# Squared-relu attention before two feed-forward blocks: key blocks in pairs, chunk sums copied out apart

## The chip, the cores and the metric

The kernel runs on one core of a Trainium2 chip. The metric is the device time of one execution in microseconds (us); a difference of under 0.2% between two kernels is about what these measurements cannot tell from none.

## The reference

```python
scores = (1.0 / S) * np.matmul(z, z.transpose(0, 2, 1))   # z: 2 x 3008 x 64
attn = np.maximum(scores, 0.0) ** 2
x = u * np.matmul(attn, v)                                # u, v: 2 x 3008 x 256, fp32
x = x.reshape(6016, 256)
h = np.maximum(x @ w_in, 0.0);  x = h * h @ w_out         # 256 -> 2048 -> 256
h = x @ w2_in;  g = h - np.tanh(h);  y = g @ w2_out       # 256 -> 2048 -> 256
```

The weights of the two feed-forward blocks are float64, the rest is float32.

## The kernel before, in words

Every operand of a matmul is split into a rounded part (hi) and a remainder (lo), both in the type fp32r, and a product is three matmuls: hi by hi, lo by hi, hi by lo. The split of an activation is two passes: a cast or copy that writes hi, and a subtraction that writes lo.

Queries are cut into 12 chunks: per batch five of 512 and one of 448. The work is a list `steps`, and a step of attention is one chunk with one block of 128 keys (24 blocks a chunk, 288 steps; the last block has 64 keys, which lie twice, in the upper and in the lower 64 rows). Then come 192 steps "m1" and 192 steps "m2", for the first and the second feed-forward block (a chunk with 128 of the 2048 hidden columns): 21 of m1, then m2 and m1 in turn, at the end m2 alone. TensorE's array is split in attention into two halves of 64 rows that work side by side, on two blocks in the scores and on the two halves of a block's keys in the values. I call two such matmuls side by side a slot. A pair of blocks has 3 slots of scores and 12 of values.

`front(i)` does the first half of step i. For attention it computes the scores of two blocks at each even step (`two_scores`, L309), takes relu (L371) and square (L372) on ScalarE, makes hi by a cast on VectorE (L385) or, for every third block, on ScalarE (L381), and lo by a subtraction on VectorE (L386, L382). `back(n)` does the second half: for attention it adds the block's values to four sums, `o`, one PSUM bank each (L462): two halves of the rows by two halves of the 256 columns. After a chunk's last block it joins the sums. For each half d of the columns ScalarE copies one bank (L484), VectorE adds the other (L485) and multiplies by u (L486), and a DMA stores the result. The pool `po` has just these four banks, so that the next chunk's first matmuls wait until a bank has been read.

The order on every engine is written out by hand, in one loop: `front(n + LOOK)`, then `back(n)`, with LOOK = 3. Each engine works its queue off in this order.

Operands that have to be loaded and split (v, z, the weights, the stored x) are units in three `Lane`s. A unit has the step at which it is needed and one from which it may be loaded. `due(n)` forces what step n needs, `fill(n, k)` puts up to k passes between the passes of a step, and `pace(n)` works out k from what is left and when it is needed (at most 2 per block in attention, 4 in m1). A weight unit takes nine passes, six of them on VectorE (L181 to L194), a v unit two, a z unit four. All split v and weights live in the pool `wp` (32 buffers of 4 KB per partition, 24 of them first for v). PSUM has eight banks: four for `o`, four single ones for scores and hidden columns (`ps`).

Of the kernel before, what the change touches and what calls it, by code (L numbers as in the profile page):

```python
# [9 lines left out]
F32 = mybir.dt.float32  # L10
F32R = mybir.dt.float32r
# [22 lines left out]
def kernel(  # L34
# [8 lines left out]
    w2_out: bass.AP,  # L43
    yT: bass.AP,
):

# [35 lines left out]
    halves = (slice(0, DQK), slice(DQK, P))  # L82
# [14 lines left out]
    at = {s: i for i, s in enumerate(steps)}  # L97

    wt = {}
    zt = {}  # L100
# [160 lines left out]
    for b in range(B):  # L261
        base, end = at["att", b * NC, 0], at["att", (b + 1) * NC - 1, 0]
        for j in range(NV):
            w_units.append((base + 2 * j, load_v, split_v, (b, j), 2))
            free_w.append(end + 2 * j + 2)
        for t in range(NC):
            z_units.append((base + 4 * t, load_z, split_z, (b, t), 4))
            free_z.append(end + min(4 * t + 4, KB))
    for m in range(2):
        for f in range(NF):  # L270
            w_units.append((at[("m1", "m2")[m], 0, f], load_w, split_w, (m, f), 9))

    for units, free, slots, first in ((w_units, free_w, NW, 1), (z_units, free_z, NZ, 0)):
        for i, u in enumerate(units):
            start = free[i - slots] + LOOK if i >= slots else 1 if i == first + 1 else 0
            units[i] = (u[0], start, *u[1:])
    for c in range(NCH):
        need = at["m1", c, 0]
# [15 lines left out]


    pair = {}
    acc = {}
    score = {}

    def two_scores(i):  # L300

        for j in (i, i + 1):
            score[j] = ps.tile([P, NMAX], F32, tag="s", name="s")
        for t, (hk, hq) in enumerate(((0, 0), (1, 0), (0, 1))):
            for g, rows in enumerate(halves):
                _, c, k = steps[i + g]
                b, q, n = chunks[c]

                T.matmul(  # L309
                    score[i + g][:, :n],  # L310
                    lhsT=zt[b, k // 4][rows, hk ^ g, (k % 4) * P : (k % 4 + 1) * P],
                    rhs=zt[b, q // NMAX][rows, hq ^ g, :n],
                    start=t == 0,
                    stop=t == 2,
                )
    late = deque()
    calm = [0]
    for kind, _, _ in steps:
# [14 lines left out]
    def interleave(n, main, k):  # L333
# [10 lines left out]
            late.popleft()()  # L344
        fill(n, k)

    def front(i):
        kind, c, k = steps[i]
        b, q, n = chunks[c]
        if kind == "att":  # L350
            if i % 2 == 0:
                two_scores(i)
            s = score.pop(i)
        else:
            s = ps.tile([P, NMAX], F32, tag="s", name="s")
        a = ap_.tile([P, NMAX], F32, tag="a", name="a")
        s_, a_ = s[:, :n], a[:, :n]
        h = hp.tile([P, NMAX], F32R, tag="hi", name="hi")
        pair[i] = (h,)
        if kind != "att" or k < KB - 1:  # L360
            l = hp.tile([P, NMAX], F32R, tag="lo", name="lo")
            pair[i] = (h, l)
        if kind == "att":
            if k == 8:
                xt[c] = xp.tile([P, KD, NMAX], F32, tag="x", name="x")
                t0 = b * S + q
                SP.dma_start(
                    out=xt[c][:, :, :n],
                    in_=uT[:, t0 : t0 + n].rearrange("(k p) t -> p k t", p=P),
                )  # L370
            A.activation(a_, s_, AF.Relu, scale=scale)  # L371
            A.activation(a_, a_, AF.Square)  # L372
            if k == KB - 1:

                up = slice(TAIL, P)
                main = [
                    lambda: V.tensor_copy(h[:, :n], a_),
                    lambda: V.tensor_sub(h[up, :n], a[up, :n], h[up, :n]),
                ]
            elif k % 3 == 1 and c > 0:  # L380
                A.activation(h[:, :n], a_, AF.Copy)  # L381
                main = [lambda: V.tensor_sub(l[:, :n], a_, h[:, :n])]  # L382
            else:
                main = [
                    lambda: V.tensor_copy(h[:, :n], a_),  # L385
                    lambda: V.tensor_sub(l[:, :n], a_, h[:, :n]),  # L386
                ]
            interleave(i, main, 2 if c == 0 else min(1 + (k + 1) % 2, pace(i)))
            return
        m = 0 if kind == "m1" else 1  # L390
        w = wt["w", m, k]
        xh, xl = xs[m, c]
# [44 lines left out]
    def back(i):  # L437
        kind, c, k = steps[i]
        b, q, n = chunks[c]
        nk = KB if kind == "att" else NF  # L440
        if k == 0:
            acc[kind] = [
                po.tile([P, NMAX], F32, tag="o", name="o")
                for _ in range(KD * (2 if kind == "att" else 1))
            ]
        o = acc[kind]
        if kind == "att":
            w, c0 = wt["v", b, k // 2], (k % 2) * D
        else:
            w, c0 = wt["w", 0 if kind == "m1" else 1, k], KD * P  # L450
        got = pair.pop(i)
        terms = [(0, got[0]), (1, got[0])]
        if len(got) == 2:
            terms.append((0, got[1]))
        seq = [(j, d) for j in range(len(terms)) for d in range(KD)]
        if k in (0, nk - 1):
            seq.sort(key=lambda x: x[1])
        for j, d in seq:
            hl, mv = terms[j]
            if kind == "att":  # L460
                for g, rows in enumerate(halves):
                    T.matmul(  # L462
                        o[g * KD + d][:, :n],
                        lhsT=w[rows, hl, c0 + d * P : c0 + (d + 1) * P],
                        rhs=mv[rows, :n],
                        start=k == 0 and j == 0,
                        stop=k == nk - 1 and j == len(terms) - 1,
                    )
                continue
            T.matmul(  # L470
                o[d][:, :n],
                lhsT=w[:, hl, c0 + d * P : c0 + (d + 1) * P],
                rhs=mv[:, :n],
                start=k == 0 and j == 0,
                stop=k == nk - 1 and j == len(terms) - 1,
            )
        if k < nk - 1:
            return
        t0 = b * S + q
        if kind == "att":  # L480
            x = xt.pop(c)
            for d in range(KD):
                t = tp.tile([P, NMAX], F32, tag="t", name="half")
                A.activation(t[:, :n], o[d][:, :n], AF.Copy)  # L484
                V.tensor_add(t[:, :n], o[KD + d][:, :n], t[:, :n])  # L485
                V.tensor_mul(x[:, d, :n], t[:, :n], x[:, d, :n])  # L486
            SP.dma_start(out=xd[c, :, :, :n], in_=x[:, :, :n])
        elif kind == "m1":
            xh, xl = new_xs(1, c)
            for d in range(KD):  # L490
                A.activation(xh[:, d, :n], o[d][:, :n], AF.Copy)
                V.tensor_sub(xl[:, d, :n], o[d][:, :n], xh[:, d, :n])
        else:
            y = xp.tile([P, KD, NMAX], F32, tag="x", name="y")
            for d in range(KD):
                if d == 0 or c < NCH - 1:
                    A.activation(y[:, d, :n], o[d][:, :n], AF.Copy)
                else:
                    V.tensor_copy(y[:, d, :n], o[d][:, :n])
                if c == NCH - 1:  # L500
                    SP.dma_start(out=yT[d * P : (d + 1) * P, t0 : t0 + n], in_=y[:, d, :n])
            if c < NCH - 1:
                SP.dma_start(
                    out=yT[:, t0 : t0 + n].rearrange("(k p) t -> p k t", p=P), in_=y[:, :, :n]
                )


    with tc.manual_schedule():
        for n in range(-LOOK, len(steps)):
            i = n + LOOK  # L510
            if i < len(steps):
                due(i)
                front(i)
            while i >= len(steps) and late:
                late.popleft()()
            if n >= 0:
                back(n)


# [34 lines left out]
```

## Time and profile before

| | |
|---|---|
| time, 3 runs | 1584.35, 1586.05, 1586.63 us, median 1586.05 |
| profiled execution | 1589.54 us, its span 1587.5 us |
| TensorE (PE) busy | 1550.9 us, 98% |
| VectorE (DVE) busy | 1235.3 us, 78% |
| ScalarE (ACT) busy | 1150.8 us, 72% |
| mean granted TensorE clock | 0.983 |

The time of an execution is its span and some 2 us around it. PE is busy while any matmul is in flight, also at a lower clock. Of the engines' names, PEld is TensorE's loading of weights, SP the queue that issues most DMAs. "[1.67 <-ACT half L484]" behind an instruction is the idle time of its engine just before it and what ended it.

### The profile page before, as it was taken

How to read it: one execution, taken by the hardware profiler on the slowest of the kernel's cores; microseconds unless marked ns; L12 is line 12 of the kernel's file. 1: busy time of each engine (PE TensorE's matmuls, PEld its weight loads, DVE VectorE, ACT ScalarE, POOL GpSimd, SP SyncE). 2: the span in 40 equal slices, each digit the busy share in tenths (PEclk: the TensorE clock that was granted, in tenths of full speed). 3: DMA queues.
4: the chain of work that ended last, by engine and by line, in shares of the span. 5: the costliest groups of instructions: out<-in, count | busy, mean ns of one | idle time of the engine just before them, and what ended most of it. 6: DMA issues, size and time to landing. Idle time of an engine off the chain costs nothing.

```text
span 1587.5 us, 23868 instructions
## 1 busy us (share of the span) xinstructions
PE 1550.9 (98%) x8880; PEld 1295.7 (82%) x8880; DVE 1235.3 (78%) x2161; ACT 1150.8 (72%) x2032; POOL 24.2 (2%) x25
## 2 busy tenths in 40 slices
PE   8999999999999999999999999999999999999998
PEld 6777878777777978888888888888888888888887
DVE  7777767787756778987778788877778787778788
ACT  7788978888877867776766666666666676666676
POOL 0000000000000000000000000000000000000014
PEclk9999999999999999999999999999999999999999
DMA  4331003222000321000000000000000000000000
GB/s 127 113 101 54 15 28 95 69 67 67 28 27 2 105 92 54 1 27 1 16 10 1 27 1 27 1 27 1 25 1 27 1 26 1 1 14 1 14 1 25
DMA packets 32772, 52.38 MB, mean 33 GB/s; under 512 B 2960, under 2 KB 19600, under 8 KB 32656
## 3 DMA queue, kind: packets, MB, share of 16 engines
q1 hardware_dynamic: 32496, 50.60, 9.8%
q8 instruction: 69, 1.13, 0.3%
q14 instruction: 47, 0.39, 0.1%
q10 hardware_dynamic: 160, 0.26, 0.1%
HBM read 38.54 MB, written 12.32 MB: 32 GB/s over the span
## 4 chain that ended last, share of the span: by engine, by line
PE 89%; DVE 6%; ACT 4%; issue 1%; DMA 0%; SPq 0%; DVEq 0%; ACTq 0%
PE s L395 31%; PE o L470 31%; PE o L462 21%; PE s L309 6%; ACT a L371 1%; ACT a L372 1%; DVE half L485 1%; DVE a L427 1%; DVE lo L386 1%; DVE f L424 1%; DVE hi L385 0%; DVE x L486 0%; DVE a L420 0%; ACT hi L381 0%; DVE vw L127 0%
## 5 line engine op out<-in xcount | busy, mean ns | idle before, releaser
L462 PE MATMUL o<-hi,vw 64*128 64x512 f32 (+1 forms) x2304 | 399.0, 400 | 23.1 <-ACT half L484 13.8
L470 PE MATMUL o<-hi,ww 128*128 128x512 f32 (+1 forms) x1536 | 413.3, 386 | 2.6 <-ACT half L484 1.6
L395 PE MATMUL s<-xh,ww 128*128 128x512 f32 (+1 forms) x1536 | 405.1, 386 | 0.0
L462 PEld LDWEIGHTS o<-hi,vw 64*128 64x128 f32 x2304 | 286.8, 193 | 77.5 <-ACT half L484 21.8
L470 PEld LDWEIGHTS o<-hi,ww 128*128 128x128 f32 x1536 | 288.2, 188 | 57.6 <-ACT half L484 2.1
L395 PEld LDWEIGHTS s<-xh,ww 128*128 128x128 f32 x1536 | 288.1, 188 | 54.8 <-issue 0.6
L403 ACT ACTIVATE a<-s 128x512 f32<-128x512 f32 (+1 forms) x192 | 113.2, 589 | 189.2 <-PE s L395 187.8
L462 PE MATMUL o<-lo,vw 64*128 64x512 f32 (+1 forms) x1104 | 247.6, 393 | 0.1
L470 PE MATMUL o<-lo,ww 128*128 128x512 f32 (+1 forms) x768 | 241.3, 385 | 0.2 <-POOL lo L435 0.2
L410 DVE TENSOR_TENSOR lo<-a,hi 128x512 fp32r<-128x512 f32 (+1 forms) x192 | 130.6, 680 | 137.2 <-ACT hi L408 136.5
L395 PE MATMUL s<-xl,ww 128*128 128x512 f32 (+1 forms) x768 | 233.4, 385 | 0.0
L371 ACT ACTIVATE a<-s 128x512 f32<-128x512 f32 (+1 forms) x288 | 166.5, 578 | 70.0 <-PE s L309 59.3
L416 ACT ACTIVATE f<-s 128x512 f32<-128x512 f32 (+1 forms) x192 | 112.9, 588 | 120.7 <-PE s L395 120.7
L372 ACT ACTIVATE a<-a 128x512 f32<-128x512 f32 (+1 forms) x288 | 179.6, 624 | 9.4
L462 PEld LDWEIGHTS o<-lo,vw 64*128 64x128 f32 x1104 | 163.6, 190 | 19.5 <-DVE lo L386 1.2
L309 PE MATMUL s<-z 64*128 64x512 f32 (+1 forms) x864 | 165.8, 406 | 7.1 <-ACT z L145 4.6
L470 PEld LDWEIGHTS o<-lo,ww 128*128 128x128 f32 x768 | 144.0, 188 | 28.2 <-POOL lo L435 0.8
L395 PEld LDWEIGHTS s<-xl,ww 128*128 128x128 f32 x768 | 144.2, 188 | 26.9
L427 DVE COPY_PREDICATED a<-small,f 128x512 f32<-128x512 uint8 (+1 forms) x192 | 147.1, 766 | 6.2
L420 DVE TENSOR_TENSOR a<-s,a 128x512 f32<-128x512 f32 (+1 forms) x192 | 130.1, 677 | 15.3 <-ACT a L417 9.7
L309 PEld LDWEIGHTS s<-z 64*128 64x128 f32 x864 | 117.7, 198 | 23.3 <-ACT z L145 4.6
L424 DVE TENSOR_TENSOR f<-s,f 128x512 f32<-128x512 f32 (+1 forms) x192 | 130.7, 681 | 6.6
(47 smaller groups left out, 1458.8 us busy)
## 6 DMA issues: line engine op xcount, KB each, us to landing
wraw<-in_moe_w_in_dram SPq DMA_DIRECT2D x32, 256.0 KB, 2.9
wraw<-in_moe_w_out_dram SPq DMA_DIRECT2D x32, 256.0 KB, 3.2
vraw<-in_v_dram SPq DMA_DIRECT2D x22, 256.0 KB, 2.8
x<-in_u_dram SPq DMA_DIRECT2D x10, 512.0 KB, 4.8
xd<-x SPq DMA_DIRECT2D x10, 512.0 KB, 3.0
xr<-xd SPq DMA_DIRECT2D x10, 512.0 KB, 3.3
out_dram<-y SPq DMA_DIRECT2D x10, 512.0 KB, 2.8
zraw<-in_z_dram SPq DMA_DIRECT2D x18, 128.0 KB, 3.9
```

The lines of the kernel that those rows point to most:

```text
L309: T.matmul(score[i + g][:, :n], lhsT=zt[b, k // 4][rows, hk ^ g, (k % 4) * P : (k % 4 + 1) * P], rhs=zt[b, q // NMAX][rows, hq ^ g, :n], s ...
L371: A.activation(a_, s_, AF.Relu, scale=scale)
L372: A.activation(a_, a_, AF.Square)
L395: T.matmul(s_, lhsT=w[:, hl, kd * P : (kd + 1) * P], rhs=mv[:, kd, :n], start=j == 0, stop=j == len(seq) - 1,)
L403: A.activation(a_, s_, AF.Relu)
L410: main.append(lambda: V.tensor_sub(l[:, :n], a_, h[:, :n]))
L416: A.activation(f_, s_, AF.Tanh, scale=TB)
L420: lambda: V.tensor_sub(a_, s_, a_),
L424: lambda: V.tensor_mul(f_, s_, f_),
L427: late.append(lambda: V.copy_predicated(a_, small_, f_))
L462: T.matmul(o[g * KD + d][:, :n], lhsT=w[rows, hl, c0 + d * P : c0 + (d + 1) * P], rhs=mv[rows, :n], start=k == 0 and j == 0, stop=k == nk ...
L470: T.matmul(o[d][:, :n], lhsT=w[:, hl, c0 + d * P : c0 + (d + 1) * P], rhs=mv[:, :n], start=k == 0 and j == 0, stop=k == nk - 1 and j == le ...
```

## The change

A step of attention is now a pair of blocks (12 a chunk, 144 in all). The scores of a pair go to one tile of two PSUM banks, and one relu, one square, one cast (always on VectorE) and one subtraction work on both blocks (1024 elements per partition). The loop first emits the scores and relu of step n+2, then the values of step n, then square, cast and subtraction of step n+2. The last block's values take 3 slots in place of 4: one half of the array does one half of the columns.

After a chunk's last pair, ScalarE copies two banks into one tile and VectorE the other two into a second, at once; the addition of the two tiles and the multiplication by u go into the list `late`, whose entries are put ahead of the passes of the next pair's split (`interleave`, unchanged). The four tiles of this kind come from `wp`, of which 7 buffers are kept for them and for the pairs' tiles; therefore 12 weight units are now loaded ahead of the second batch's v, and of the other 20 one may be loaded when the first batch's v is freed, and 19 only from the last chunk of attention on. In m1 and m2, scores' banks and hi and lo are pair tiles of the same total size.

```diff
 LOOK = 3
+APART = 2
-READY = 3
+READY = 2
+NTEMP = 7
-    ps = ctx.enter_context(tc.tile_pool(name="ps", bufs=4, space=bass.MemoryType.PSUM))
+    ps = ctx.enter_context(tc.tile_pool(name="ps", bufs=2, space=bass.MemoryType.PSUM))
-    steps = [("att", c, k) for c in range(NCH) for k in range(KB)]
+    steps = [("att", c, p) for c in range(NCH) for p in range(NV)]
...
+    early = NW - NTEMP - NV - 1
+    w_units[NV:NV] = weights[:early]
+    w_units += weights[early:]
+    free_w += [at["m1", 0, 0]] * NTEMP
+    for units, free, slots, first in ((w_units, free_w, NW - NTEMP, 1), (z_units, free_z, NZ, 0)):
         for i, u in enumerate(units):
+            start = free[i - slots] + APART + 1 if i >= slots else 1 if i == first + 1 else 0
...
+    def scores(i):
...
+        s = ps.tile([P, 2, NMAX], F32, tag="s", name="s")
...  (six matmuls, as in two_scores)
+        a = wp.tile([P, 2, NMAX], F32, tag="w", name="a2")
+        A.activation(a[:, :, :n], s[:, :, :n], AF.Relu, scale=scale)
+        return a
+
+    def squares(i, a):
...
+        h = hp.tile([P, 2, NMAX], F32R, tag="h", name="h2")
+        l = wp.tile([P, 2, NMAX], F32R, tag="w", name="l2")
+        A.activation(a, a, AF.Square)
+        main = [
+            lambda: V.tensor_copy(h[:, :, :n], a),
+            lambda: V.tensor_sub(l[:, :, :n], a, h[:, :, :n]),
+        ]
+        interleave(i, main, min(5, pace(i)) if c else 4)
+
+    def values(i):
...
+        terms = ((0, h), (1, h), (0, l))
+        order = [(g, d, d) for g in range(2) for d in range(KD)]
+        if last:
+            order = [(1, 0, 1), (0, 0, 0), (0, 1, 1)]
...  (for each entry of order, for each term: one matmul per half of the rows)
+        e = [wp.tile([P, KD, NMAX], F32, tag="w", name="e") for _ in range(2)]
+        for d in range(KD):
+            A.activation(e[0][:, d, :n], o[d][:, :n], AF.Copy)
+            V.tensor_copy(e[1][:, d, :n], o[KD + d][:, :n])
+        def join():
+            V.tensor_add(e[0][:, :, :n], e[0][:, :, :n], e[1][:, :, :n])
+        def gate():
+            V.tensor_mul(x[:, :, :n], e[0][:, :, :n], x[:, :, :n])
+            SP.dma_start(out=xd[c, :, :, :n], in_=x[:, :, :n])
+        late.append(join)
+        late.append(gate)
...
-        for n in range(-LOOK, len(steps)):
-            i = n + LOOK
-            if i < len(steps):
+        for n in range(-1, len(steps)):
+            until = n + (APART if n + APART < at["m1", 0, 0] else LOOK)
+            todo = []
+            while ahead <= min(until, len(steps) - 1):
+                i, ahead = ahead, ahead + 1
                 due(i)
-                front(i)
+                if steps[i][0] == "att":
+                    todo.append((i, scores(i)))
+                    if i < APART:
+                        squares(*todo.pop())
+                else:
+                    front(i)
...
             if n >= 0:
-                back(n)
+                (values if steps[n][0] == "att" else back)(n)
+            for x in todo:
+                squares(*x)
```

## Rows read from the trace of the kernel before

**Rows 1.** The page: busy time and share of the span by engine.
```profile
PE 1550.9 (98%) x8880; PEld 1295.7 (82%) x8880; DVE 1235.3 (78%) x2161; ACT 1150.8 (72%) x2032; POOL 24.2 (2%) x25
```
**Rows 2.** TensorE's waits over the whole span: us in total, times, longest.
```profile
PE o L462 <- ACT half L484: 13.8, 11, 2.3
PE o L462 <- DVE half L485: 8.6, 12, 0.9
...
PE o L470 <- ACT half L484: 1.6, 1, 1.6
```
**Rows 3.** Chain that ended last, in time: start us, us, what.
```profile
124.54 0.68 PE s L309 x6
125.22 2.72 PE o L462 x24
...
257.25 2.07 PE o L462 x20
260.35 2.07 PE o L462 x20
...
547.98 1.60 PE s L395 x6
```
**Rows 4.** Timeline, TensorE: the start, the next chunk's first values, the end of attention.
```profile
4.58 3.27 PE L309 MATMUL s<-z 64*128 64x512 f32 x12 [4.58 <-ACT z L145]
...
14.21 1.22 PE L309 MATMUL s<-z 64*128 64x512 f32 x4 [2.47 <-DVE z L147]
...
59.09 1.21 PE L462 MATMUL o<-hi,vw 64*128 64x512 f32 x4 [2.26 <-ACT half L484]
...
556.51 1.19 PE L395 MATMUL s<-xh,ww 128*128 128x512 f32 x4
```
**Rows 5.** Timeline where the second chunk gives way to the third.
```profile
105.08 1.06 ACT L484 ACTIVATE half<-o 128x512 f32<-128x512 f32 x2
...
105.71 1.21 PE L462 MATMUL o<-hi,vw 64*128 64x512 f32 x4 [1.67 <-ACT half L484]
...
108.48 1.22 PE L462 MATMUL o<-hi,vw 64*128 64x512 f32 x3 [0.83 <-DVE half L485]
```
**Rows 6.** Windows: length, busy us (count) of PE, PEld, DVE, ACT, POOL; granted clock, DMA share, GB/s.
```profile
60.00:108.00 48.00, 45.27 (x362) 36.72 (x358) 34.62 (x63) 40.52 (x72) 0.00 (x0) 0.93 0.28 87
...
200.00:245.00 45.00, 43.04 (x356) 34.87 (x356) 28.20 (x49) 34.19 (x59) 0.00 (x0) 0.96 0.08 25
...
109.00:110.00 1.00, 1.00 (x8) 0.72 (x6) 0.35 (x2) 0.00 (x0) 0.00 (x0) 0.50 0.00 0
...
560.00:561.00 1.00, 1.00 (x5) 0.82 (x5) 0.97 (x3) 0.97 (x3) 0.00 (x0) 1.00 0.00 0
```
**Rows 7.** Groups by line and shape: count, busy us, mean ns, idle before.
```profile
L386 DVE TENSOR_TENSOR lo<-a,hi 128x512 fp32r<-128x512 f32 x158 | 108.9, 689 | 7.3
...
L385 DVE CAST hi<-a 128x512 fp32r<-128x512 f32 x158 | 67.2, 425 | 52.0 <-ACT a L372 42.1 <-PE o L462 7.8 <-ACT a L371 1.0
...
L386 DVE TENSOR_TENSOR lo<-a,hi 128x448 fp32r<-128x448 f32 x30 | 18.7, 622 | 1.3
...
L385 DVE CAST hi<-a 128x448 fp32r<-128x448 f32 x30 | 11.7, 391 | 8.4 <-ACT a L372 7.0 <-PE o L462 1.1
...
L209 ACT ACTIVATE xh<-xr 128x1024 fp32r<-128x1024 f32 x10 | 10.4, 1044 | 0.0
```
**Rows 8.** Timeline in the stage where m2 and m1 alternate.
```profile
1001.13 1.07 PE L395 MATMUL s<-xh,ww 128*128 128x512 f32 x4
...
1004.87 0.69 DVE L424 TENSOR_TENSOR f<-s,f 128x512 f32<-128x512 f32 x1
...
1008.87 0.98 PE L395 MATMUL s<-xh,ww 128*128 128x448 f32 x4
```
**Rows 9.** Windows of line L194, a weight unit's last pass: busy us (count), clock, DMA.
```profile
559.00:604.00 45.00, 3.42 (x5) 1.00 0.30 97
604.00:650.00 46.00, 2.05 (x3) 1.00 0.09 31
```

More of the change, by code (lines that the diff above doesn't have):

```diff
@@ L97 @@
     at = {s: i for i, s in enumerate(steps)}
+    halves = (slice(0, DQK), slice(DQK, P))
     wt = {}
@@ L296 @@
     pair = {}
+    two = {}
     acc = {}
[L298 to L315, printed above, removed]
     late = deque()
@@ L345, in interleave @@
         fill(n, k)
+    def scores(i):
+        _, c, p = steps[i]
+        b, q, n = chunks[c]
+        if p == 4:
+            xt[c] = xp.tile([P, KD, NMAX], F32, tag="x", name="x")
+            t0 = b * S + q
+            SP.dma_start(
+                out=xt[c][:, :, :n],
+                in_=uT[:, t0 : t0 + n].rearrange("(k p) t -> p k t", p=P),
+            )
+        s = ps.tile([P, 2, NMAX], F32, tag="s", name="s")
+        for t, (hk, hq) in enumerate(((0, 0), (1, 0), (0, 1))):
+            for g, rows in enumerate(halves):
+                k = 2 * p + g
+                T.matmul(
+                    s[:, g, :n],
+                    lhsT=zt[b, k // 4][rows, hk ^ g, (k % 4) * P : (k % 4 + 1) * P],
+                    rhs=zt[b, q // NMAX][rows, hq ^ g, :n],
+                    start=t == 0,
+                    stop=t == 2,
+                )
+        a = wp.tile([P, 2, NMAX], F32, tag="w", name="a2")
+        A.activation(a[:, :, :n], s[:, :, :n], AF.Relu, scale=scale)
+        return a
@@ new lines, in squares @@
+    def squares(i, a):
+        _, c, p = steps[i]
+        n = chunks[c][2]
+        a = a[:, :, :n]
+        h = hp.tile([P, 2, NMAX], F32R, tag="h", name="h2")
+        l = wp.tile([P, 2, NMAX], F32R, tag="w", name="l2")
+        pair[i] = (h, l)
+        A.activation(a, a, AF.Square)
+        main = [
+            lambda: V.tensor_copy(h[:, :, :n], a),
+            lambda: V.tensor_sub(l[:, :, :n], a, h[:, :, :n]),
+        ]
+        interleave(i, main, min(5, pace(i)) if c else 4)
+    def values(i):
+        _, c, p = steps[i]
+        b, q, n = chunks[c]
+        if p == 0:
+            acc["att"] = [po.tile([P, NMAX], F32, tag="o", name="o") for _ in range(2 * KD)]
+        o = acc["att"]
+        w = wt["v", b, p]
+        h, l = pair.pop(i)
+        terms = ((0, h), (1, h), (0, l))
+        last = p == NV - 1
+        order = [(g, d, d) for g in range(2) for d in range(KD)]
+        if last:
+            order = [(1, 0, 1), (0, 0, 0), (0, 1, 1)]
+        started, left = set(), [x for g, *ds in order for x in enumerate(ds)]
+        for g, *ds in order:
+            for j, (hl, mv) in enumerate(terms):
+                for r, rows in enumerate(halves):
+                    d = ds[r]
+                    if j == 0:
+                        left.remove((r, d))
+                    T.matmul(
+                        o[r * KD + d][:, :n],
+                        lhsT=w[rows, hl, g * D + d * P : g * D + (d + 1) * P],
+                        rhs=mv[rows, g, :n],
+                        start=p == 0 and j == 0 and (r, d) not in started,
+                        stop=last and j == 2 and (r, d) not in left,
+                    )
+                    started.add((r, d))
+        if not last:
+            return
+        x = xt.pop(c)
+        e = [wp.tile([P, KD, NMAX], F32, tag="w", name="e") for _ in range(2)]
[9 more added lines that the diff above has]
+        late.append(gate)
@@ L451, in back @@
[L451 to L454, printed above, removed]
+        w = wt["w", 0 if kind == "m1" else 1, k]
+        hl = pair.pop(i)
+        terms = ((0, hl[:, 0, :n]), (1, hl[:, 0, :n]), (0, hl[:, 1, :n]))
         seq = [(j, d) for j in range(len(terms)) for d in range(KD)]
-        if k in (0, nk - 1):
+        if k in (0, NF - 1):
             seq.sort(key=lambda x: x[1])
         for j, d in seq:
[L459 to L469, printed above, removed]
+            side, mv = terms[j]
```

93 lines of the change are left out of this document (22 added, 71 removed).

## The prediction

> **What bounds the kernel now.** I read the busy line of the profile's page first: PE is busy 98% of the span, DVE 78%, ACT 72% [rows 1]. Busy means "a matmul is in flight", so the next question is at which rate PE works. The chain gives it. In undisturbed attention the chain is PE alone, 0.68 us of scores and 2.72 us of values in turn [rows 3]. That is 3.40 us for 15 slots, 0.2267 us a slot; a pair of the 448-wide chunks comes every 260.35 - 257.25 = 3.10 us, 0.2067 a slot [rows 3]. There, a faster DVE or ACT is worth nothing.
>
> How much of attention is like that? A chunk has 36 slots of scores, 23 x 6 + 4 of values, 178 in all. Ten chunks of 512 need 1780 x 0.2267 = 403.5 us and two of 448 need 356 x 0.2067 = 73.6, together 477.1. The first matmul starts at 4.58; the first m1 matmul behind attention's last values starts at 556.51 [rows 4]; between lie three pieces of m1 of 1.6 us each (the first is the last row of [rows 3]). So attention takes 556.51 - 4.58 - 4.8 = 547.1 us. **It loses 70.0 us.** The rest of this text is where they go.
>
> The first chunk: the second one's values start at 59.09, 54.5 us after the first matmul [rows 4]. Until then there are 178 + 6 slots, 41.7 us. It loses 12.8, of which 2.26 is the wait that stands at this row; 10.5 are its own. The other 70.0 - 10.5 = 59.5 us belong to 11 passages from chunk to chunk, **5.4 us each**. The list of waits names the cause: PE waits for `half`, for ACT's copy 13.8 us and for DVE's addition 8.6 us, 11 or 12 times each, with one more of 1.6 us at m1's first values [rows 2]. One passage in time: PE waits 1.67 us for the first copies, does four matmuls, and soon waits 0.83 more for the second addition [rows 5], which stands behind the multiplication of the first half in DVE's queue. The waits are 2.0 us per passage. The clock adds to it: right after the second wait the granted clock is 0.50, the lower level of 1.2 GHz in the window from 109 to 110 [rows 6]. The windows of 45 to 48 us that hold one passage show 0.93 to 0.96, the first two lines of [rows 6], so 1.8 us (0.04 x 45) to 3.4 us (0.07 x 48) of time at full rate are lost there. The remainder of the 5.4 is thin flow before the wait and refilling after it.
>
> **The change, part by part.**
>
> *Wide passes.* No trace shows them at 1024 on DVE; each lies between one and two passes of 512. By the slope between 512 and 448 [rows 7] a subtraction takes 0.689 + 512 x (0.689 - 0.622)/64 = 1.22 us, a cast 0.425 + 512 x (0.425 - 0.391)/64 = 0.70. ACT's 1024-wide copy takes 1.04 [rows 7], and I take this for relu and square. A pair then costs DVE 1.92 us and ACT 2.08, under PE's 3.40. In the undisturbed stretch this is worth nothing. What it changes is latency: relu, square, cast, subtraction are 1.04 + 1.04 + 0.70 + 1.22 = 4.0 us from the scores' end to the end of lo. Its cover is PE's work until lo's first use, the third slot of the pair's values: values, scores, values, scores and two slots, 2.72 + 0.68 + 2.72 + 0.68 + 0.45 = 7.25 us. 3.2 us are spare; zero.
>
> *One slot less per chunk.* 10 x 0.2267 + 2 x 0.2067 = **-2.7 us**.
>
> *The passage.* Time 0 is the start of a chunk's last values (9 slots, 2.04 us); the scores of the next chunk's second pair, n+2, are just done. ACT: its relu until 1.04; the copies (0.53 each by the pair of [rows 5]) of the banks that are full at 1.36 and at 2.04, until 2.57; square until 3.61. DVE: its copies read PSUM, which no row shows for a plain copy of 512; they lie between the cast's 0.43 and the subtraction's 0.69 [rows 7], and I take 0.69, as for other PSUM readers: until 2.73. PE: scores until 2.72, then the next chunk's first values, whose banks are read by then. So the old wait is gone, at both halves. What is late next is lo of pair n+2: `interleave` puts the join ahead of its cast and the multiplication ahead of its subtraction. DVE: join 2.73 to 3.95, cast to 4.65, multiplication to 5.87, subtraction to 7.09. PE wants this lo at 2.72 + 2.72 + 0.68 + 0.45 = 6.57: a wait of 0.52 us. For the refilling I add 0.33, an estimate: the four matmuls behind a wait take 1.21 [rows 5] where two slots are 0.45, but a part of this is the flight of the last matmul. Bounds: 0 (DVE's copies at 0.43) to 1.8 us (one or two weight passes of 0.69 in front, full refilling). I take 0.85, eleven times: 9.4. I let the clock stay up. For it speaks that a wait of 1.6 us at m1's start [rows 2] is followed by a clock of 1.00, the last line of [rows 6]; against it, the 0.50 after two waits. So **-59.5 + 9.4 = -50.1 us**; the wait at m1 goes too, **-1.6**, since the three m1 pieces before the last values are put there by PE's order and the copies end 0.7 us after those values, under 1.36 us of the next hidden columns.
>
> The Trainium skill, in "TensorE: Matmul & The Clock Gate", section "A second HAM failure mode: psum-queue depth-cycling", holds that short idles between matmul groups that cycle through PSUM banks are enough to make the clock swing. By it the new waits would keep the loss of clock, and the sum would be 20 to 37 us worse; by the row at m1's start it would not. I weigh this as a rival.
>
> *The start.* PE's queue now has the third pair's scores ahead of the first values. These need the second z unit, on which PE waits until 14.21 now [rows 4], with the values of two blocks done before. These 12 slots move behind the wait, 2.7 us, and the wait ends later, since up to four wide passes stand before z's on DVE: 1.7 us, an estimate from their lengths. Some of the chunk's other losses may go. I take **+2**, between -2 and +6.
>
> *Weights.* Nineteen units are left for the time from the last chunk on. In attention at most 5 passes go with each of six pairs, in the 21 m1 steps 4 each: (30 + 84 - 3)/9 = 12.3 units, so that some 6.7 units fall into the m2 stage, 4 passes per m2-and-m1 pair. Before, five were finished in the m1 stage and three in the 46 us after [rows 9]. A pair takes PE 24 x 0.2267 = 5.44 us. DVE has seven passes of its own, 5 x 0.69 + 2 x 0.43 = 4.3, and 2.7 weight passes of 0.6 (two of six cast-like, four like the subtraction): 5.9. Over 16 pairs it falls behind by up to 7 us, of which part lies in the lead of three steps. **+2**, between 0 and 8.
>
> *Free edits.* Two steps share a tile of scores in m1 and m2, so m1's front waits for the m2 step three before. That one's last reader ends at 1004.87 + 0.69 = 1005.56, and the m1 matmuls start at 1008.87 [rows 8]: 3.3 us spare in each of 171 places. SP issues the same DMAs, one store per chunk; weights loaded earlier or later find it idle nearly always.
>
> **Sum.** -2.7 - 50.1 - 1.6 + 2 + 2 = -50.4 us. The profiled execution took 1589.5, so its like would take 1539.1; the median of the runs is 3.5 lower, and from it the forecast is 1586.05 - 50.4 = **1536 us**.
>
> **Rivals.**
> 1. *The clock still falls at each passage*, because PE still waits. Price 11 x 1.8 to 11 x 3.4 us, 20 to 37 (mean 28): 1564. The 0.50 of [rows 6] speaks for it, the 1.00 behind 1.6 us of waiting against it. 13%.
> 2. *Slower: a pair's chain outgrows its cover.* ACT and DVE work in order, up to five passes of other work go with a pair, and the pair's tiles must find one of 7 buffers free. Each us beyond 7.25 costs every one of 132 pairs that us. It decides from 50.4/132 = 0.38 us beyond, that is 3.6 us of other work in each chain, five or six passes of 0.69. At 1 us beyond: 1536 + 132 = 1668. Against it: the limit of five is asked for only where many units are due. 4%.
> 3. *No change: the wait only moves.* If join and multiplication held lo back for about 5 us per passage, all would be as before, 1586 less 4 = 1582 or so. This needs 4 us more of DVE work in front than I count. 4%.
>
> **Numbers.** The forecast has 79%, with its own range 1522 to 1552. The range of 8 in 10 takes in rival 1: the low end is no new wait and a better start (-59.5 - 2.7 - 1.6 - 2 = -65.8, 1520), hardly all at once, so 1522; the high end is rival 1 at its mean, 1564. A difference under 0.2%, about 3 us, can't be told from none. Faster 0.93 (the forecast, rival 1 and a quarter of rival 3, whose 1582 lies at the edge), same 0.03, slower 0.04.
>
> **What would show it.** In the trace after: no wait of PE for a reader of `o` beyond 0.3 us; one wait of about 0.5 us for lo, at each chunk's second pair; a granted clock of 1.00 in windows that hold a passage; attention's last values about 50 us earlier; hidden scores' wait at the start later than 14.21; PE without gaps while m2 begins. The prediction is wrong if the clock is 0.5 after the new waits, if the wait for lo is over 2 us, or if gaps of PE come with each pair.

## The result: slower, 1608 us in place of 1536

The kernel after takes **1608.45 us** (median of 4 runs, 1608.18 to 1612.57), the kernel before on the same chip 1586.34 (1584.35 to 1586.74). The ratio is **1.0148, with the interval 1.0130 to 1.0166**. The forecast was 1536, and faster.

What became of the gain is seen by laying the two traces side by side at fixed places of the work. I read from each timeline when ScalarE begins to copy a finished sum; a chunk ends there.

| ScalarE's first copy of | before, us | after, us | difference |
|---|---|---|---|
| attention, chunk 1 of 12 | 58.46 | 60.83 | +2.4 |
| attention, chunk 11 | 511.55 | 468.42 | -43.1 |
| attention, chunk 12 | 559.23 | 521.92 | -37.3 |
| m1, chunk 1 | 603.77 | 567.37 | -36.4 |
| m1, chunk 2 | 675.88 | 654.32 | -21.6 |
| m2, chunk 1 | 700.70 | 701.07 | +0.4 |
| m2, chunk 10 | 1473.87 | 1474.24 | +0.4 |
| m2, chunk 11 | 1547.60 | 1553.71 | +6.1 |
| m2, chunk 12 | 1583.36 | 1602.33 | +19.0 |

So 43 us are there after eleven chunks, and are then lost in three places: 6 in attention's last chunk, 37 while m2 begins, 19 at the end, where m2 steps run alone.

The windows of the trace after (columns as in [rows 6]) show the same from inside:

```profile
60.00:105.00 45.00, 44.51 (x394) 36.52 (x392) 37.06 (x50) 34.60 (x41) 0.00 (x0) 1.00 0.16 54
200.00:245.00 45.00, 44.23 (x412) 38.26 (x410) 37.48 (x52) 33.83 (x42) 0.00 (x0) 1.00 0.20 62
465.00:510.00 45.00, 38.82 (x347) 32.74 (x344) 30.86 (x44) 28.66 (x36) 0.00 (x0) 0.98 0.27 93
510.00:555.00 45.00, 43.15 (x199) 34.24 (x198) 37.58 (x72) 28.90 (x49) 0.00 (x0) 0.95 0.28 92
...
605.00:655.00 50.00, 42.61 (x174) 33.77 (x173) 42.15 (x76) 31.45 (x57) 0.00 (x0) 0.93 0.13 42
655.00:705.00 50.00, 36.68 (x130) 28.60 (x129) 30.67 (x53) 23.80 (x41) 0.00 (x0) 0.83 0.04 12
705.00:1500.00 795.00, 795.00 (x3559) 668.13 (x3558) 629.94 (x1072) 530.48 (x935) 0.00 (x0) 1.00 0.03 12
1500.00:1606.00 106.00, 85.67 (x389) 71.69 (x387) 78.14 (x126) 60.46 (x120) 23.61 (x20) 1.00 0.03 10
```

The first two windows, in attention, run as hoped: PE busy over 98%, the granted clock 1.00 where [rows 6] had 0.93 and 0.96. From 705 to 1500 nothing is lost at all. The bad stretches are 465 to 555, 605 to 705 and 1500 to the end. In the trace before, the stretch in which m2 begins was full:

```profile
605.00:655.00 50.00, 50.00 (x222) 41.40 (x222) 46.02 (x83) 36.97 (x65) 0.00 (x0) 1.00 0.07 23
655.00:705.00 50.00, 50.00 (x222) 41.42 (x221) 43.02 (x75) 35.07 (x62) 0.00 (x0) 1.00 0.03 11
```

The clock is seen best in the 8 us behind the start of a passage's copies, here of one passage, in the trace before and then in the trace after:

```profile
105.10:113.10 8.00, 6.56 (x35) 4.57 (x37) 5.58 (x10) 3.89 (x8) 0.00 (x0) 0.79 0.40 131
...
101.70:109.70 8.00, 7.52 (x67) 5.86 (x66) 7.82 (x10) 7.26 (x9) 0.00 (x0) 1.00 0.32 97
```

Over all eleven passages it is 0.59 to 0.79 before and 1.00 after. For the ten up to chunk 11, what each is short of 1.00, times 8 us, sums to some 22 us (an estimate): about half of the 43 is the clock.

TensorE's list of waits in the trace after (columns as in [rows 2]) gives the bad stretches names:

```profile
PE s L448 <- DVE f L477: 16.6, 10, 2.3
PE s L448 <- ACT ww L198: 15.9, 3, 5.7
PE s L448 <- ACT a L456: 9.4, 8, 2.7
PE s L358 <- ACT z L150: 9.1, 2, 4.7
PE o L407 <- DVE l L380: 7.8, 13, 1.0
PE s L358 <- DVE z L152: 5.1, 2, 2.6
PE s L448 <- DVE ww L199: 2.6, 1, 2.6
```

The waits for `half` of [rows 2] are gone. In their place stands the short wait for lo, L380. But L448 (the scores of m1 and m2) has three new ones: for `ww`, a weight unit; for `a`, the relu of an m1 step; for `f`, the last multiplication of an m2 step, ten times, all behind 1500.

**The passage, in time.** The timeline of the trace after where the third chunk gives way to the fourth; it answers to [rows 5]:

```profile
142.68 1.28 ACT L420 ACTIVATE e<-o 128x512 f32<-128x512 f32 x2 [0.32 <-PE o L407]
142.71 1.37 DVE L421 COPY e<-o 128x512 f32<-128x512 f32 x2
...
143.16 0.84 PE L358 MATMUL s<-z 64*128 64x512 f32 x6
143.84 0.62 PE L407 MATMUL o<-h,vw 64*128 64x512 f32 x4
...
144.19 1.23 DVE L424 TENSOR_TENSOR e<-e 128x1024 f32<-128x1024 f32 x1
...
145.33 0.69 DVE L379 CAST h<-a 128x1024 fp32r<-128x1024 f32 x1
...
145.93 1.22 DVE L427 TENSOR_TENSOR x<-e,x 128x1024 f32<-128x1024 f32 x1
...
147.07 1.22 DVE L380 TENSOR_TENSOR l<-a,h 128x1024 fp32r<-128x1024 f32 x1
...
148.34 0.50 PE L407 MATMUL o<-l,vw 64*128 64x512 f32 x2 [0.48 <-DVE l L380]
```

Both engines copy at once, and PE's first values of the next chunk (from 143.84) follow the scores ahead of them without any wait. Then join, cast, multiplication and subtraction follow on DVE as worked out, 1.23, 0.69, 1.22 and 1.22 us, and PE waits 0.48 us for lo, where 0.52 was forecast.

**The onset of m2.** A weight unit that the planner has put off until the very step that needs it:

```profile
670.19 0.42 DVE L186 TENSOR_SCALAR mant<-wraw 128x512 uint32<-128x512 uint32 x1
...
670.65 0.63 ACT L188 ACTIVATE mant<-mant 128x512 f32<-128x512 uint32 x1 [1.55 <-DVE mant L186]
670.86 0.69 DVE L190 SCALAR_TENSOR_TENSOR mant<-wraw,mant 128x512 f32<-128x512 uint32 x1
671.47 0.69 DVE L193 SCALAR_TENSOR_TENSOR exp<-wraw,exp 128x512 uint32<-128x512 uint32 x1
672.19 0.69 DVE L196 TENSOR_TENSOR mant<-mant,exp 128x512 f32<-128x512 f32 x1
672.91 0.63 ACT L198 ACTIVATE ww<-mant 128x512 fp32r<-128x512 f32 x1 [1.63 <-DVE mant L196]
...
673.59 2.08 PE L448 MATMUL s<-xh,ww 128*128 128x512 f32 x4 [5.70 <-ACT ww L198]
```

The passes of one unit run one after another, from DVE to ACT and back, 3.4 us from the first to the one that PE wants, and PE stands 5.70. Then its four matmuls take 2.08 us, where undisturbed ones take 1.07 [rows 8], and the granted clock is 0.50 from 673.6 to 678.0: the lower clock is the second part of the price. From 600 to 700 the waits sum to 22.0 us (15.9 and 2.6 for `ww`, 3.5 for `a`), and the granted clock of 0.93 and 0.83 in two windows of 50 us costs some 3.5 and 8.5 us more, an estimate (50 us times what is short of 1.00).

**The tail.** m2 steps alone, near the end:

```profile
1574.88 1.08 PE L448 MATMUL s<-xh,ww 128*128 128x448 f32 x4 [1.56 <-DVE f L477]
1575.80 0.56 PE L448 MATMUL s<-xl,ww 128*128 128x448 f32 x2
1576.20 1.38 PE L504 MATMUL o<-h,ww 128*128 128x448 f32 x6
1577.42 0.97 PE L448 MATMUL s<-xh,ww 128*128 128x448 f32 x4
...
1581.65 1.09 PE L448 MATMUL s<-xh,ww 128*128 128x448 f32 x4 [1.63 <-DVE f L477]
```

Every second step waits: two steps take 1581.65 - 1574.88 = 6.77 us. In the trace before two such steps took 1565.61 - 1560.75 = 4.86, without a wait:

```profile
1560.75 0.97 PE L395 MATMUL s<-xh,ww 128*128 128x448 f32 x4
...
1563.18 0.97 PE L395 MATMUL s<-xh,ww 128*128 128x448 f32 x4
...
1565.61 0.98 PE L395 MATMUL s<-xh,ww 128*128 128x448 f32 x4
```

### The profile page after: what moved, and what is told of

It reads as the page before. It is cut to its first block, busy times and chain, and to the rows that moved or that the text cites. A ratio compares the mean times of both kernels' runs of the same rounds, so it can differ in the third digit from the quotient of the medians.

```text
span 1606.5 us, 22511 instructions
## 1 busy us (share of the span) xinstructions
PE 1532.1 (95%) x8856; PEld 1271.4 (79%) x8856; DVE 1246.9 (78%) x1961; ACT 1063.5 (66%) x1656; POOL 23.9 (1%) x25
## 4 chain that ended last, share of the span: by engine, by line
PE 82%; DVE 12%; ACT 4%; issue 2%; DMA 0%; DVEq 0%; ACTq 0%
PE s L448 30%; PE o L504 28%; PE o L407 19%; PE s L358 5%; DVE l L380 1%; DVE f L477 1%; DVE a L473 1%; DVE h L379 1%; DVE e L421 1%; DVE a L480 1%; DVE x L427 1%; ACT a L366 1%; ACT a L377 1%; DVE small L474 1%; DVE e L424 1%
## 5 line engine op out<-in xcount | busy, mean ns | idle before, releaser
L504 PE MATMUL o<-h,ww 128*128 128x512 f32 (+1 forms) x2304 | 581.3, 388 | 2.0 <-ACT e L420 1.4
L504 PEld LDWEIGHTS o<-h,ww 128*128 128x128 f32 x2304 | 435.9, 189 | 85.8 <-ACT e L420 1.9
L448 PE MATMUL s<-xh,ww 128*128 128x512 f32 (+1 forms) x1536 | 412.1, 390 | 44.6 <-DVE f L477 16.6
L448 PEld LDWEIGHTS s<-xh,ww 128*128 128x128 f32 x1536 | 289.0, 190 | 108.1 <-DVE f L477 20.6
L407 PE MATMUL o<-h,vw 64*128 64x512 f32 (+1 forms) x2256 | 347.5, 385 | 1.8 <-DVE e L421 1.0
L407 PEld LDWEIGHTS o<-h,vw 64*128 64x128 f32 x2256 | 214.3, 186 | 43.4 <-DVE e L421 1.4
L463 DVE TENSOR_TENSOR h<-a,h 128x512 fp32r<-128x512 f32 (+1 forms) x192 | 130.6, 680 | 141.8 <-ACT h L461 141.6
L448 PE MATMUL s<-xl,ww 128*128 128x512 f32 (+1 forms) x768 | 235.8, 389 | 0.0
L456 ACT ACTIVATE a<-s 128x512 f32<-128x512 f32 (+1 forms) x192 | 112.8, 588 | 177.7 <-PE s L448 176.8
L407 PE MATMUL o<-l,vw 64*128 64x512 f32 (+1 forms) x1128 | 221.6, 387 | 7.9 <-DVE l L380 7.8
L366 ACT ACTIVATE a<-s 128x1024 f32<-128x1024 f32 (+1 forms) x144 | 144.9, 1007 | 123.6 <-PE s L358 123.5
L380 DVE TENSOR_TENSOR l<-a,h 128x1024 fp32r<-128x1024 f32 (+1 forms) x144 | 172.9, 1201 | 2.9
L448 PEld LDWEIGHTS s<-xl,ww 128*128 128x128 f32 x768 | 145.3, 189 | 27.7
L377 ACT ACTIVATE a<-a 128x1024 f32<-128x1024 f32 (+1 forms) x144 | 150.1, 1042 | 4.2
L477 DVE TENSOR_TENSOR f<-s,f 128x512 f32<-128x512 f32 (+1 forms) x192 | 130.7, 681 | 6.6
L407 PEld LDWEIGHTS o<-l,vw 64*128 64x128 f32 x1128 | 107.5, 186 | 33.6 <-DVE l L380 14.2
```

Source lines behind the costliest of these rows:

```text
L366: A.activation(a[:, :, :n], s[:, :, :n], AF.Relu, scale=scale)
L377: A.activation(a, a, AF.Square)
L380: lambda: V.tensor_sub(l[:, :, :n], a, h[:, :, :n]),
L407: T.matmul(o[r * KD + d][:, :n], lhsT=w[rows, hl, g * D + d * P : g * D + (d + 1) * P], rhs=mv[rows, g, :n], start=p == 0 and j == 0 and ( ...
L448: T.matmul(s_, lhsT=w[:, hl, kd * P : (kd + 1) * P], rhs=mv[:, kd, :n], start=j == 0, stop=j == len(seq) - 1,)
L463: main.append(lambda: V.tensor_sub(l[:, :n], a_, h[:, :n]))
```

## The experiments

They were run in four sets, each beside the kernel before on the same chip; the column "before" tells the sets apart.

| kernel | median, us | before, us | ratio, interval |
|---|---|---|---|
| after, own tiles in the tail | 1594.60 | 1586.42 | 1.0040, 1.0023 to 1.0056 |
| after, short split | 1562.56 | 1586.42 | 0.9843, 0.9827 to 0.9860 |
| before, 25 buffers | 1636.61 | 1586.42 | 1.0314, 1.0294 to 1.0335 |
| before, copies apart | 1567.15 | 1586.42 | 0.9873, 0.9858 to 0.9887 |
| own tiles, m2 12 steps behind | 1920.78 | 1589.02 | 1.2102, 1.2079 to 1.2125 |
| the same, three passes | 1919.67 | 1589.02 | 1.2093, 1.2072 to 1.2114 |
| after, own tiles, short split | 1541.70 | 1589.02 | 0.9713, 0.9696 to 0.9730 |
| before, short split | 1577.15 | 1589.02 | 0.9928, 0.9904 to 0.9951 |
| own tiles, 11 steps | 1575.16 | 1586.05 | 0.9925, 0.9906 to 0.9944 |
| own tiles, 11 steps, three passes | 1574.99 | 1586.05 | 0.9927, 0.9912 to 0.9942 |
| own tiles, 13 steps, three passes | 1565.59 | 1586.05 | 0.9869, 0.9852 to 0.9885 |
| the same, own tiles in m1 alone too | 1566.65 | 1588.88 | 0.9856, 0.9840 to 0.9872 |

### The tail: a tile of its own for each step

```diff
 def front(i):
-        if i % 2 == 0 or kind == "m1" and (c, k) == (0, 0):
+        if i % 2 == 0 or i > at["m1", NCH - 1, NF - 1]:
             two["s"] = ps.tile([P, 2, NMAX], F32, tag="s", name="s")
```

> The changed kernel, but in the last stage, where m2 runs alone, each step takes a tile of its own for its hidden columns instead of half of a shared one. Theory 'shared half' (the second step of a pair waits for all readers of the first one's half): the ten waits of 1.6 us for line L477's product go, the stage is some 18 us shorter, time about 1590 us. Rival 'the stage is bound by VectorE or GpSimd' : no change, 1608 us.

1594.60, 13.9 us less by the medians. In its trace the waits on L477 are gone, and m2's last two chunks end 73.74 and 35.79 us after the one ahead, as before (73.73 and 35.76); after had 79.47 and 48.62. That is 18.6 us in the tail; its profiled run lost 2.6 of it at the start (first chunk at 63.44) and 2.9 up to m1's first chunk, where PE waited 3.7 us for a copy of L420 that cost 1.4 in after. The mechanism holds, and with it that the wait is one for the whole tile: the second step of a tile is held up by readers of the first step's half.

### The weights: two passes in place of nine

The unit takes every second 32-bit word as if it were fp32; the conversion from float64 is left out.

```diff
 def split_w(m, f, raw):
-        if w1_in.dtype == F32:
-            val = raw
-        else:
+        if True:
+            val = raw.bitcast(F32).rearrange("p (n two) -> p n two", two=2)[:, :, 1]
+        else:
...
-        (at[("m1", "m2")[m], 0, f], load_w, split_w, (m, f), 9)
+        (at[("m1", "m2")[m], 0, f], load_w, split_w, (m, f), 2)
```

> The changed kernel, but a weight unit takes two passes instead of nine: the upper words of the float64 weights are read as float32, so the conversion is left out. Theory 'late weights' (19 units crowd ScalarE and VectorE from the last chunk of attention to the first chunk of m2, and come due one by one): the last chunk loses 10 us less and m2's start about 37 us less, time 1555 to 1567 us, and no wait of TensorE for a weight unit. Rival 'shared tiles slow m1 and m2': TensorE's waits for L456 stay and the time stays over 1590 us. By both, the 17 us of the last stage stay.

1562.56, 45.9 less than after. The waits for `ww` are gone, those for `a` are down to 0.7, attention's last chunk takes 41.7 us in place of 53.5, and PE is busy 50.00 of 50 us from 605 to 655. The tail keeps its 16.8 us of L477.

### The kernel before, with seven buffers fewer

```diff
+    free_w += [at["m1", 0, 0]] * 7
-    for units, free, slots, first in ((w_units, free_w, NW, 1),
+    for units, free, slots, first in ((w_units, free_w, NW - 7, 1),
```

> The kernel before with one part of the change alone: the planner keeps 7 of the 32 buffers back until m1 begins (they stay empty), so that 19 weight units in place of 12 are left for the time from the last chunk on. Theory 'late weights': slower than before by 35 to 50 us, 1621 to 1636 us, with waits for weight units at m2's first steps. Rival 'shared tiles slow m1 and m2': within 6 us of before, 1586 to 1592 us.

1636.61, 50 us slower than before and just past the theory's upper end. Its list of waits:

```profile
PE s L396 <- ACT ww L193: 26.8, 6, 5.8
...
PE s L396 <- DVE ww L194: 5.7, 1, 5.7
```

The buffers alone, with nothing else of the change, bring the waits for weights: it is not the pairs nor the wider passes. Attention itself became shorter: its last chunk ends at 549.43, 9.8 us earlier than before, with only 13 of the 32 weight units ahead of that chunk in place of 20. Behind it 56 us are lost until m2's first chunk ends (747.10 against 700.70).

### The kernel before, with the copies apart

```diff
+            e = [wp.tile([P, KD, NMAX], F32, tag="w", name="e") for _ in range(2)]
             for d in range(KD):
-                t = tp.tile([P, NMAX], F32, tag="t", name="half")
-                A.activation(t[:, :n], o[d][:, :n], AF.Copy)
-                V.tensor_add(t[:, :n], o[KD + d][:, :n], t[:, :n])
-                V.tensor_mul(x[:, d, :n], t[:, :n], x[:, d, :n])
-            SP.dma_start(out=xd[c, :, :, :n], in_=x[:, :, :n])
+                A.activation(e[0][:, d, :n], o[d][:, :n], AF.Copy)
+                V.tensor_copy(e[1][:, d, :n], o[KD + d][:, :n])
...  (join and gate go into late, as in after; two buffers reserved)
```

> The kernel before with another part alone: a chunk's sums are copied out at once by both engines into two tiles, and joined and multiplied later; two of the 32 buffers are kept back for these tiles, the steps stay single blocks. Theory 'the copies are the whole gain of attention': 11 passages of 4.5 us each go, two more late units cost 0 to 8 us, time 1537 to 1548 us. Rival 'the wide passes are needed for it' (join and multiplication hold back the next blocks' hi and lo, with only three blocks of lead): waits for L385 or L386 of 2 us or more per passage, 1560 to 1580 us.

1567.15, in the rival's range, but not by the rival's cause: waits for hi or lo at the passages, which it put at 2 us each, sum to 0.5 (`PE o L463 <- DVE hi L386`). The waits for DVE's half are gone, but `PE o L463 <- ACT e L485` still has 13.7 us in 11. The timeline shows what ACT does ahead of the copies:

```profile
189.24 0.60 ACT L372 ACTIVATE a<-s 128x512 f32<-128x512 f32 x1 [0.22 <-PE s L310]
189.87 0.63 ACT L373 ACTIVATE a<-a 128x512 f32<-128x512 f32 x1
190.41 1.06 ACT L485 ACTIVATE e<-o 128x512 f32<-128x512 f32 x2
...
191.04 1.21 PE L463 MATMUL o<-hi,vw 64*128 64x512 f32 x4 [0.71 <-ACT e L485]
```

Relu and square of a block further on stand in ACT's queue ahead of the copy. The copies apart, with two buffers fewer, are worth 19 us. Up to chunk 11 the trace gains 22.9 us, of after's 43.1. The other part came with the new loop, which puts the square behind the copies; that the loop does it, and not the wide passes, is read from this row and was not tested alone.

### A longer lead of m1, and what an even number does

```diff
-LAG = 5
+LAG = 12
-        free = need - 8 if c == 0 else at["m1", c - 1, 0] + 4
+        free = need - 8 if c == 0 else at["m1", c - 1, 0] + (18 if c > 2 else 4)
```

The second kernel also has `min(3, pace(i))` in place of `min(5, pace(i))` in `squares`.

> After, with a tile of scores of its own for each step of the m2 stage's end, and m2 beginning 12 steps of m1 behind instead of 5: seven more steps that carry four weight passes each lie ahead of the first m2 step, so that no weight unit is left to its due step. Theory (late weights cost the 35 us between m1's first chunk and the end of m2's first chunk): PE's waits on L198 and L199 go, and the time falls from 1594.6 by 28 to 38 us, less 1 to 2 us for seven more m2 steps that run alone: 1556 to 1568. Rival (it is not when the passes are due but how many there are: conversion and buffers are simply full, and m1 steps with four passes run slow): the 35 us move into the longer m1 stage, 1580 to 1596.

> As the kernel with m2 twelve steps behind, and besides no more than three weight passes in a pair of attention instead of five. Theory (the 12 us that attention's last chunk lost came from five passes on ACT and DVE in each pair, more than its copy, relu and square leave room for): the last chunk falls from 53 to 43 to 46 us, and the time to 1545 to 1560, 7 to 11 below the kernel with five. Rival (the passes cost the same wherever they stand, or those put off come due in m2): no difference beyond 2 us, or slower.

Both lie over 350 us above the theories' upper ends, through a cause that neither theory nor rival named. The waits for `ww` are gone, but the list begins with

```profile
PE s L448 <- DVE f L477: 284.1, 164, 4.4
```

With LAG = 5 the first m2 step has an odd number, so a shared tile holds an m1 step first and an m2 step second, and the m2 step waits for a relu, which is early. With 12 the m2 step comes first, and the m1 step waits for its multiplication, through the whole stage:

```profile
1004.84 0.69 DVE L477 TENSOR_TENSOR f<-s,f 128x512 f32<-128x512 f32 x1
...
1005.58 1.20 PE L448 MATMUL s<-xh,ww 128*128 128x512 f32 x4 [1.60 <-DVE f L477]
```

This is the tail's mechanism at full length, 1.7 us each time. The 3.3 us that the prediction found spare in each of 171 places [rows 8] were there only because 21 is odd. In attention, three passes per pair did what was expected: the last chunk takes 43.3 us, with five 48.5.

### 11 and 13 steps

```diff
-LAG = 12
+LAG = 11
```

The second kernel has three passes per pair besides, the third 13 steps (and 20 for 18).

> After, with a tile of its own for each step of the m2 stage's end, and m2 beginning 11 steps of m1 behind instead of 5; an odd number, as 5 is, so that in each shared tile the m1 step comes first and the m2 step second. With 12 the m2 step came first, and the m1 step waited 164 times (284.1 us) for the m2 step's last multiply. Theory (that was the shared tile's order alone, and late weights cost the 35 us at m2's onset): the waits on L477 go, those on L198 and L199 stay away, and the time is that expected of 12 steps: 1556 to 1568. Rival (the other waits of a longer lag, for the buffers of the split activations above all, take the place): 1580 or more.

> As the kernel with 11 steps, and no more than three weight passes in a pair of attention instead of five. With 12 steps attention's last chunk took 42 to 44 us with three and 48 with five. Theory (five passes in a pair are more than ACT and DVE have room for): 4 to 9 us below the kernel with five: 1548 to 1562. Rival (what is put off costs as much in m1's first steps): within 2 us of it.

> As the kernel with 11 steps and three passes, with 13 steps. Theory (with 11 no unit is late any more): within 3 us of it, up to 1 us more for the two further m2 steps that run alone. Rival (units that are not late by the planner's steps are still late in time, since a unit's passes run one after another on ACT and DVE): 4 us or more below it.

With an odd number the waits on L477 are gone. 11 steps give 1575.16: 19 us less than the kernel with 5, but 7 more than the theory's upper end. Three passes in attention gain 3.8 us in its last chunk. In these two traces that kernel is 8 us ahead when m1's second chunk ends (627.75 against 635.80) and no longer when m2's first one does (701.29 against 701.09): it waits 5.6 us there in two waits for `ww`, which the kernel with five passes does not have. So 1574.99, and the rival holds: passes put off cost as much later. 13 steps give 1565.59: also the rival, units that are due in time by the planner's steps are still late by the clock. The list has no `ww` any more, but 17.1 us of `PE s L448 <- ACT a L456`: a step's first matmuls wait for the relu of an m1 step before it, which stands on ACT behind a weight pass that itself waits for DVE. ACT's own list, from 505 to 705:

```profile
ACT ww L198 <- DVE mant L196: 36.7, 17, 4.3
```

### Is it the sharing that hands these delays on?

```diff
-        if i % 2 == 0 or i > at["m1", NCH - 1, NF - 1]:
+        if i % 2 == 0 or not at["m2", 0, 0] <= i <= at["m1", NCH - 1, NF - 1]:
```

> As the kernel with 13 steps and three passes, with a tile of scores of its own for each step in the stage where m1 runs alone too; only where m1 and m2 steps alternate do two share one. With shared tiles that kernel's scores there waited 12 times, 16.5 us, for a relu that stood on ACT behind a weight pass (ACT waited 36.7 us in 17 for mant). Theory (sharing is what hands these delays on: an odd step waits for the relu of the step just before, with its own tile for that of the step before that, one step of 2.7 us more): the waits on L456 fall by 8 to 14 us, and the time from 1565.6 to 1551 to 1559. Rival (the passes are more than ACT and DVE can do in such a step, and the delay comes anyway): within 3 us of 1565.6.

1566.65, within the rival's 3 us: no, where m1 runs alone. The edit halves the waits that it can reach: the six on L456 ahead of m2's first step sum to 4.7 us, with shared tiles to 9.0. But that first step, which still shares its tile, then waits 3.88 us in place of 1.16, and from the end of attention's last chunk to that of m2's first it takes 186.1 us in place of 186.3: the delay comes anyway. Another 7 us of these waits lie where m1 and m2 alternate; there both kernels share tiles, and for them the question stays open. The rival's reason, that the passes are more than ACT and DVE can do, is not shown: from 511 to 700 DVE is busy 83% and ACT 66%. What the traces show is order: ACT stands 39.2 us in 17 waits for `mant` (from 505 to 705), and the relu stands behind.

### Both costs away, and the kernel before without conversion

Both edits are those shown above: the tiles of the tail and the short split in after, the short split alone in before.

> After, with both suspected costs away: a tile of scores of its own for each step of the m2 stage's end, and the weights split in two passes, without the conversion from their stored form. Theory (the two costs are separate and explain all that was lost against the forecast): the tail's 18.9 us come off the 1562.6 of the short split alone: 1541 to 1547. Rival (the tail's waits only show because something else is late there, as the 14 us measured with the weights in place may say): 1548 to 1556.

> The kernel before, with the weights split in two passes, without the conversion from their stored form. Theory (with seven more buffers the weights cost before next to nothing but the 6 us that attention's last chunk is longer): 1576 to 1583. Rival (the weights cost before as they do after, and the short split takes that away from any kernel): 1540 to 1565, and then the gain of 46 us from the short split in after says little of the change.

After, with the tail's own tiles and the short split: **1541.70**, within the theory's bounds; before, with the short split: 1577.15. Set against each other at the places of the table above, the differences are +4.8, -33.6, -37.2, -35.9 and then -35.9 to the end: the attention gain that is left there stays, once nothing takes it back.

## Why the prediction was wrong, step by step

*The passage, -59.5 + 9.4: right in its mechanism, and in its size partly by luck.* From chunk 1 to chunk 11 a chunk takes (511.55 - 58.46)/10 = 45.31 us before and (468.42 - 60.83)/10 = 40.76 after, 4.55 less. Forecast were 5.4 - 0.85 and a slot of 0.23, so 4.8. A chunk with nothing special in it takes 101.74 - 60.83 = 40.91 us, where 177 slots need 40.12: a passage still loses 0.8, where 0.85 was forecast. But the 5.4 held some 0.75 per passage that was weight passes and not the copies (see "The rest" below). One wait for a copy stayed, 0.99 us at the passage to the second batch.

*The clock stays up: right, and rival 1 fell.* Granted clock 1.00 in the 8 us behind each of the eleven passages, with a wait of 0.5 to 1.0 us in each. The Trainium skill, in "TensorE: Matmul & The Clock Gate", section "A second HAM failure mode: psum-queue depth-cycling", tells of a kernel in which frequent short idles between groups of matmuls that cycle through PSUM banks swung the clock; these passages, one in 41 us, do not show it.

*The start, +2: right*, +2.4 in this trace (up to +5.3 in those of the experiments). The scores that need the second z unit now wait until 16.33, where [rows 4] has 14.21. Two further waits for z, 4.48 us until 12.38 and 2.56 until 27.69, are new and were not in the forecast. Since the chunk ends only 2.4 later, they take the place of time that it lost elsewhere before.

*m1's first wait, -1.6: wrong by its whole size.* `PE o L504 <- ACT e L420` is 1.4 us. With the short split it is not among the waits, so the copies came late behind weight passes. The same split takes the 1.6 out of the kernel before, too.

*Weights, +2, between 0 and 8: the step that failed first.* The count was near: eight units end after m2's first tanh at 576.04, some of them begun before, against 6.7. The price was wrong. I took the passes as load on DVE, spread over 16 pairs, and asked how far DVE falls behind. But a unit not done at its step is done there at once, its passes one after another on two engines, and PE stands, up to 5.70 us, with its clock halved behind it. In attention's last chunk five passes in a pair held up lo, relu and values: of 53.5 us, some 12 are lost (with the short split the chunk takes 41.7), 7.6 of them in waits between 460 and 525 and some 3.6 at a mean clock of 0.93 from 470 to 522 (an estimate). Together the weights cost 45.9 us (short split) in after, where before pays 11.9, so the change added 34 where +2 was forecast; the kernel before with 25 buffers is 50 us slower.

*Free edits, 0: the step that failed second.* "3.3 us spare in each of 171 places" was read in the stage where m2 and m1 alternate and is true there. The other 21 m2 steps, which run alone, I did not look at. There the step that shares the tile is an m2 step too, and the wait for its multiplication costs 18.6 us.

*The rest.* With both costs away the time is 1541.70, 7.7 above the 1536 - 2 that the forecast would be without its weights. But the short split helps the kernel before as well, to 1577.15. So the change as such is worth 35.5 us, where the sum without its weights had 52.4. Some of what I put down to the passages was weight passes beside them: with the short split a chunk before takes 44.56 on the mean, not 45.31, 7.5 us over ten, and its last chunk 45.4 in place of 47.7. Another 2.8 are the start, +4.8 in these two traces, and 1.6 is m1's first wait, which neither of the two has. The remaining 2.7 or so I cannot place.

*The rivals.* None was the one that came. The slower rival had the right kind of cause (other passes in a pair's chain, too few buffers) but in the wrong place: not in 132 pairs of attention, but in its last 12 and in the first 16 m2 steps.

**A version that beats both.** Own tiles in the tail, 13 steps and three passes: 1565.59, 0.9869 of before. It is still 24 us above the kernel without the conversion. Since before pays 11.9 for the conversion too, some 12 of them are what the seven buffers still cost by pushing work behind attention.

## What to carry to other kernels

When buffers are taken from a loader, price the last units at the step where they are due: as a chain of their passes with the consumer idle, not as a share of an engine's load. When two steps come to share one tile, the second waits for all readers of the first, so go through each stage for which step comes second, also the short stage at the end, and through its parity. An average with idle time on DVE and ACT (DVE 28 to 29 of 45 us busy in each window from 315 to 450 here) says nothing of whether a unit may start: it was buffers, not engines, that were full.

## What the runs showed of the hardware that was not expected

Waits that look alike were followed by different clocks. The timeline of TensorE in the last kernel of the table (undisturbed, such a group of four takes 1.07 us):

```profile
613.77 1.20 PE L448 MATMUL s<-xh,ww 128*128 128x512 f32 x4 [0.26 <-ACT a L456]
...
633.50 1.20 PE L448 MATMUL s<-xh,ww 128*128 128x512 f32 x4 [1.49 <-ACT a L456]
...
647.03 1.99 PE L448 MATMUL s<-xh,ww 128*128 128x512 f32 x4 [2.35 <-ACT a L456]
```

The first two cost themselves and 0.13 us more; behind the third the group took nearly twice as long, and the granted clock was 0.52 from 647 to 650. But the length of the wait does not decide it. In the kernel with 11 steps and three passes a longer wait stands before a group at full clock (1.00 from 520 to 530):

```profile
520.17 1.20 PE L448 MATMUL s<-xh,ww 128*128 128x512 f32 x4 [3.20 <-ACT a L456]
```

With 13 steps and three passes, 2.32 us were followed by 1.19 and 3.25 by 2.07. What sets the two apart, these traces do not show. Nor did many short waits bring the lower clock: the kernel with 12 steps waited 164 times, 284.1 us in all, PE was busy 77 to 78% in four windows of 249 to 300 us from 705 to 1853, and its mean granted clock was 0.98.
